# Weight residues on GpSimd, normed y on ScalarE, and one state layout for both heads of a pair

## The chip, the cores and the metric

The kernel runs on one core of a Trainium2 chip. A core has five engines with queues of their own: TensorE (PE, with PEld for its weight loads), VectorE (DVE), ScalarE (ACT), GpSimd (POOL) and SyncE (SP), which here issues the transfers. Engines wait for each other by semaphores, and each takes its own instructions in the order in which the program lists them. The metric is the device time of one execution in microseconds, as the median of a few runs.

## The reference

Three layers follow each other, all in float32. In the program the weights arrive as 64-bit words and are first turned into float32.

```python
# attention, for every batch b (4) and head h (8), over t = 0..767, head size 48
state = alpha[:, :, t, :, None] * state + einsum('bhd,bhe->bhde', k[:, :, t], v[:, :, t])
y[:, :, t] = einsum('bhd,bhde->bhe', q[:, :, t], state)
# x: the heads side by side, 3072 tokens x 384
xn = x / sqrt(mean(x * x) + 1e-06) * rms_g
g = xn @ w_gate                                  # 384 x 1536
x = (g * sigmoid(g) * (xn @ w_val)) @ w_out      # 1536 x 384
h = maximum(maximum(x @ w1, x @ w2), x @ w3)     # 384 x 768 each
return h @ w2_out                                # 768 x 384
```

## The kernel before

**Attention.** The 768 tokens of a batch are cut into 6 chunks c of 128; with 4 batches that makes 24 tiles (class `Tile_`), numbered n, chunk by chunk over the batches. In a tile the 8 heads lie in 4 pairs: one head of a pair on partitions 0 to 47, the other on 64 to 111. For the first six tiles PE transposes alpha, k and q (part `pa`, `pe_a`, line 570); later ones come in already cut so that DVE transposes them (`bt`). DVE forms running products of alpha by scans and scales k and q with them (`br`, `b`). PE makes the scores (`pb`, line 644, one PSUM bank for each head of a pair), DVE masks them (`c`, line 657), and PE forms the new state U (line 667) and y (part `pc`): from the old state by line 676, and from the masked scores by line 682. Tiles with c = 0 have no old state. The scaled old state `Sd` is 96 columns wide, with each head of the pair in its own half of the rows and of the columns and zeros elsewhere, so that one matmul of 112 rows serves both heads. ScalarE sums the squares of y (`ss`), POOL forms r = (mean + eps)^-0.5 (`rr`, lines 693 and 696), DVE updates the state (`st`) and makes the normed y, xn = y * r * g (`d`, line 710), PE transposes it (`pd`), and it is split into a high part xh (ScalarE, `eh`) and a residue xl (DVE, `el`).

**The split.** Every product of the two later layers is three matmuls in the fp32r type: high x high, high x residue, residue x high. A weight chunk of 128 x 384 (class `Weights`) is loaded by SP as 64-bit words, joined to float32 by three DVE instructions (lines 58 to 60), copied to its high part by ScalarE (`high`, line 374), and the residue is the difference of the two (`low`, line 380, on DVE). ScalarE also checks the range of the words (lines 389 and 392). There are 60 chunks, taken two at a time.

**Layers.** Blocks of 384 tokens (three tiles) go through the feed-forward layer in slots: gate and value products (line 760), their product on DVE (line 793), its split, and the second matmul (line 807). The last layer follows in the same way (lines 760 and 960).

**Order.** Nothing is ordered by hand: class `Order` simulates the engines with a cost and a due time for each part, and lists the instructions in the order in which its model starts them. Where its PE would stand idle ahead of the value product of slot 0 it places a dummy matmul (`fill`, line 767). After slot 0 has begun, three PSUM banks are left for attention. `ident`, the unit matrix that the transposes need, and `mask` are built on POOL by helpers (masks.py).

Of the kernel before, what the change touches and what calls it, by code (L numbers as in the profile page):

```python
# [11 lines left out]
F32 = mybir.dt.float32  # L12
# [6 lines left out]
ALU = mybir.AluOpType  # L19
# [262 lines left out]
def gla_moe_moe(ctx: ExitStack, tc: tile.TileContext, q, k, v, alpha, wg, wv, wo, g, w1, w2, w3, wo2, out):  # L282
# [27 lines left out]
    banks = [pp.tile([P, 512], F32, name=f"bank{i}") for i in range(8)]  # L310
# [11 lines left out]
    class Weights:  # L322


        def __init__(self, tag, pool, bufs, chunks, where, due, needs):

            self.tag, self.pool, self.raws, self.tmps = tag, pool, {}, {}
            self.chunks, self.where = chunks, where
            n = len(chunks)
            first = tag == "w1"  # L330
            for i in range(n):
                at = due(i) - 10 - (HEAD[i // 2] if first and i < 8 else 1.5)
                before = needs(i) + self.prev("load", i, 1) + self.prev("check", i, bufs)
                if i >= bufs:
                    before.append((tag, "join", (i - bufs) // 2 * 2))
                plan.add((tag, "load", i), "SP", 1.1, at, before, partial(self.load, i, bufs), later=LAT)
            for i in range(0, n, 2):
                both = [j for j in (i, i + 1) if j < n]
                at = due(i) - (HEAD[i // 2] if first and i < 8 else 1 if first else 1.5)
                plan.add((tag, "join", i), "DVE", 1.3 * len(both), at,  # L340
                         [(tag, "load", j) for j in both] + self.prev("rest", i, 2) + self.prev("join", i, 2),
                         partial(self.join, both))
                plan.add((tag, "high", i), "ACT", 0.42 * len(both), at, [(tag, "join", i)] + self.needed(needs, both),
                         partial(self.high, both))
                plan.add((tag, "rest", i), "DVE", 0.47 * len(both), at + 0.2, [(tag, "high", i)],
                         partial(self.low, both))
                for j in both:
                    plan.add((tag, "check", j), "ACT", 1.14, at + 2, [(tag, "load", j)],
                             partial(self.check, j))
# [81 lines left out]
    gb = ap1.tile([P, DM], F32, name="gb")  # L431
# [10 lines left out]
    Sds = [ap1.tile([W, NP, 2 * D], F32, name=f"Sd{s}") for s in range(2)]  # L442
    for t in (ends, starts, *Sds):
        nc.gpsimd.memset(t, 0.0)
# [3 lines left out]
    make_identity(nc, ident)  # L448
    make_upper_triangular(nc, mask, val=1.0, diag=True)
# [19 lines left out]

    def square(col, src, rows, n):  # L470
        nc.scalar.activation(junk[:rows, :n], src, AF.Square, accum_out=stats[:rows, col:col + 1])
# [4 lines left out]
    class Tile_:  # L476


        def __init__(self, n):
# [36 lines left out]
            add("br", "DVE", 1.6, 1, [t("pa" if self.pe else "bt")] + free, self.pre_br)  # L516
            add("b", "DVE", 2.1 if c else 1.8, 1, [t("br")] + ([t("st", n - B)] if c else []) +
                ([t("st", n - 2)] if n < NT - B + 2 else []), self.pre_bq)
            add("sqb", "ACT", 1.48, 1.5, [t("b")], self.post_b)
# [4 lines left out]
            add("c", "DVE", 1.25, 2, [t("pb"), t("pc", n - 1)], self.pre_c)  # L524
# [3 lines left out]
            add("ss", "ACT", 0.42, 3, [t("pc")], self.norm)  # L528
            add("rr", "POOL", 0.6, 3, [t("ss")], self.root)
            if not last:  # L530
                add("st", "DVE", 0.54, 3, [t("pc")], self.pre_st)
# [3 lines left out]
            add("eh", "ACT", 0.42, 4, [t("pd")], self.split_h)  # L535
            add("el", "DVE", 0.47, 4, [t("eh")], self.split_l)
# [93 lines left out]
        def pe_b(self):  # L630
            self.in_b = []
            self.sc = []
# [5 lines left out]
            for _ in HALVES:  # L638
                sc, j = take(self.n, P, NP, P)
                self.in_b.append(j)  # L640
                self.sc.append(sc)
            for pr in range(NP):
                for i, lo, hi in HALVES:
                    nc.tensor.matmul(  # L644
                        self.sc[i][:, pr, :], self.kT[lo:hi, pr, :], self.qT[lo:hi, pr, :], start=True, stop=True
                    )
# [6 lines left out]
        def pre_c(self):  # L653
            self.at = []
            for i in range(2):
                a_ = ap.tile([P, NP, P], F32, name="at", bufs=2)
                nc.vector.tensor_tensor(a_, self.sc[i], mask.unsqueeze(1).to_broadcast([P, NP, P]), ALU.mult)
                self.at.append(a_)
            give(self.in_b[-2:])

        def pe_c(self):
            vt, at = self.vt, self.at
            if self.c < NC - 1:
                self.U, self.in_u = take(self.n, W, NP, D)
                for pr in range(NP):
                    for i, lo, hi in HALVES:
                        nc.tensor.matmul(  # L667
                            self.U[lo:hi, pr, :], self.kn[:, pr, lo:hi], vt[:, 2 * pr + i, :],
                            start=True, stop=True, skip_group_check=True,
                        )  # L670

            self.y, self.in_y = take(self.n, P, H, D)
            for pr in range(NP):
                if self.c:
                    for tk in TOKENS:
                        nc.tensor.matmul(  # L676
                            self.y[tk, 2 * pr:2 * pr + 2, :].rearrange("p a d -> p (a d)"), self.qT[:, pr, tk],
                            Sds[self.s][:, pr, :], start=True, stop=False, skip_group_check=True,
                        )
                for i in range(2):  # L680
                    for tk in TOKENS:
                        nc.tensor.matmul(  # L682
                            self.y[tk, 2 * pr + i, :], at[i][:, pr, tk], vt[:, 2 * pr + i, :],
                            start=not self.c, stop=True, skip_group_check=True,
                        )
            self.y = self.y.rearrange("p h d -> p (h d)")

        def norm(self):
            square(self.c0 + 3, self.y, P, DM)
# [8 lines left out]
        def pre_st(self):  # L698
            for i, lo, hi in HALVES:
                if self.c:  # L700
                    nc.vector.tensor_tensor(
                        St[self.b][lo:hi], self.U[lo:hi], Sds[self.s][lo:hi, :, i * D:(i + 1) * D], ALU.add
                    )
                else:
                    nc.vector.tensor_copy(St[self.b][lo:hi], self.U[lo:hi])
# [12 lines left out]
        def split_h(self):  # L718
# [4 lines left out]
            nc.scalar.activation(xh[blk][:, :, j * P:(j + 1) * P], self.xt, AF.Copy)  # L723

        def split_l(self):
            sl = slice(self.j * P, (self.j + 1) * P)
            nc.vector.tensor_tensor(
                xl[self.blk][:, :, sl], self.xt, xh[self.blk][:, :, sl].bitcast(F32), ALU.subtract
            )
            give([self.in_d])  # L730

    def give(which):
        for i in which:
# [3 lines left out]
             lambda: nc.sync.dma_start(out=gb, in_=g.unsqueeze(0).to_broadcast([P, DM])), later=2.0)  # L737
# [312 lines left out]
```

## Time and profile before

| | us |
|---|---|
| median of 3 runs | 926.93 (926.07 to 927.68) |
| the profiled execution | 927.05 |
| its span | 925.2 |
| PE busy | 888.6 |
| DVE busy | 527.4 |
| ACT busy | 353.4 |
| POOL busy | 24.3 |

Busy time is the time in which an engine has at least one instruction under way. A matmul's record is longer than the time after which the next may start, so the distance of two starts says more than a duration. The clock in a table of windows is what PE was granted there: 1.00 is 2.4 GHz and 0.50 is 1.2 GHz. The rows on which the prediction rests stand further below.

### The profile page before, as it was taken

How to read it: one execution, taken by the hardware profiler on the slowest of the kernel's cores; microseconds unless marked ns; L12 is line 12 of the kernel's file. 1: busy time of each engine (PE TensorE's matmuls, PEld its weight loads, DVE VectorE, ACT ScalarE, POOL GpSimd, SP SyncE). 2: the span in 40 equal slices, each digit the busy share in tenths (PEclk: the TensorE clock that was granted, in tenths of full speed). 3: DMA queues.
4: the chain of work that ended last, by engine and by line, in shares of the span. 5: the costliest groups of instructions: out<-in, count | busy, mean ns of one | idle time of the engine just before them, and what ended most of it. 6: DMA issues, size and time to landing. Idle time of an engine off the chain costs nothing.

```text
span 925.2 us, 16299 instructions
## 1 busy us (share of the span) xinstructions
PE 888.6 (96%) x6477; PEld 864.7 (93%) x6477; DVE 527.4 (57%) x1052; ACT 353.4 (38%) x898; POOL 24.3 (3%) x70
## 2 busy tenths in 40 slices
PE   4899699899999999999999999999999999999997
PEld 3789699799999999999999999999999999999997
DVE  3999978987666666666666258465333323323222
ACT  3568577432333333333223258553222212212121
POOL 1001000000000000000000000000000000000000
PEclk9999799999999999999999999999999999999999
DMA  8745454533223223222221025221100101101000
GB/s 170 130 125 172 129 187 120 146 108 82 56 57 82 57 56 83 56 57 82 57 56 53 1 86 182 92 99 39 52 26 27 52 1 52 39 13 52 1 26 28
DMA packets 106241, 69.14 MB, mean 75 GB/s; under 512 B 49200, under 2 KB 103856, under 8 KB 106160
## 3 DMA queue, kind: packets, MB, share of 16 engines
q1 hardware_dynamic: 106160, 68.05, 26.8%
q8 instruction: 52, 0.85, 0.4%
q14 instruction: 29, 0.24, 0.1%
HBM read 57.41 MB, written 10.62 MB: 74 GB/s over the span
## 4 chain that ended last, share of the span: by engine, by line
PE 84%; DVE 7%; DMA 2%; ACT 1%; issue 1%; POOL 0%; SPq 0%; DVEq 0%; POOLq 0%; ACTq 0%
PE bank L760 53%; PE bank L807 14%; PE bank L960 8%; PE bank L644 2%; PE bank L682 2%; PE bank L676 2%; DMA raw<-in_moe_w_dram 1%; DMA raw<-in_moe_w_val_dram 1%; PE bank L667 1%; DVE cv_t L59 1%; PE bank L716 1%; DVE aT L611 1%; DVE cv_t L60 1%; PE bank L637 1%; DVE sg L793 1%
## 5 line engine op out<-in xcount | busy, mean ns | idle before, releaser
L945 DVE TENSOR_TENSOR sg<-sg,bank 128x384 f32<-128x384 f32 x96 | 53.2, 554 | 171.6 <-PE bank L760 168.3
L793 DVE TENSOR_TENSOR sg<-sg,bank 128x384 f32<-128x384 f32 x96 | 52.8, 551 | 104.2 <-PE bank L760 103.5
L797 ACT ACTIVATE hh<-sg 128x384 fp32r<-128x384 f32 x96 | 50.2, 523 | 150.6 <-DVE sg L793 150.5
L760 PE MATMUL bank<-xh,wvh 128*128 128x384 f32 x288 | 98.7, 343 | 7.3 <-DVE sg L793 4.3
L760 PE MATMUL bank<-xh,wgh 128*128 128x384 f32 x288 | 100.8, 350 | 0.0
L760 PE MATMUL bank<-xh,wvl 128*128 128x384 f32 x288 | 97.7, 339 | 1.6 <-DVE wvl L380 1.6
L760 PE MATMUL bank<-xh,wgl 128*128 128x384 f32 x288 | 97.2, 337 | 1.5 <-DVE wgl L380 1.5
L807 PE MATMUL bank<-hh,woh 128*128 128x384 f32 x288 | 98.5, 342 | 0.0
L807 PE MATMUL bank<-hl,woh 128*128 128x384 f32 x288 | 96.7, 336 | 1.8 <-DVE hl L801 1.8
L760 PE MATMUL bank<-xl,wvh 128*128 128x384 f32 x288 | 97.4, 338 | 0.0
L760 PE MATMUL bank<-xl,wgh 128*128 128x384 f32 x288 | 97.1, 337 | 0.0
L807 PE MATMUL bank<-hh,wol 128*128 128x384 f32 x288 | 96.4, 335 | 0.0
L949 ACT ACTIVATE hh<-sg 128x384 fp32r<-128x384 f32 x48 | 25.2, 525 | 160.2 <-DVE sg L945 160.2
L801 DVE TENSOR_TENSOR hl<-sg,hh 128x384 fp32r<-128x384 f32 x96 | 53.3, 555 | 32.1 <-ACT hh L797 32.1
L790 ACT ACTIVATE sg<-bank 128x384 f32<-128x384 f32 x96 | 46.6, 486 | 47.2 <-PE bank L760 46.7
L760 PEld LDWEIGHTS bank<-xh,wvh 128*128 128x128 f32 x288 | 54.8, 190 | 9.8 <-DVE sg L793 6.4
L760 PEld LDWEIGHTS bank<-xh,wvl 128*128 128x128 f32 x288 | 54.9, 191 | 2.2 <-DVE wvl L380 2.2
L807 PEld LDWEIGHTS bank<-hl,woh 128*128 128x128 f32 x288 | 54.1, 188 | 2.7 <-DVE hl L801 2.7
L760 PEld LDWEIGHTS bank<-xh,wgl 128*128 128x128 f32 x288 | 54.6, 190 | 1.8 <-DVE wgl L380 1.8
L807 PEld LDWEIGHTS bank<-hh,woh 128*128 128x128 f32 x288 | 54.2, 188 | 2.0
L760 PEld LDWEIGHTS bank<-xh,wgh 128*128 128x128 f32 x288 | 54.8, 190 | 1.3
L760 PEld LDWEIGHTS bank<-xl,wvh 128*128 128x128 f32 x288 | 54.9, 191 | 0.0
(137 smaller groups left out, 2004.3 us busy)
## 6 DMA issues: line engine op xcount, KB each, us to landing
raw<-in_moe_w_out_dram SPq DMA_DIRECT2D x18, 384.0 KB, 3.9
raw<-in_moe_w_dram SPq DMA_DIRECT2D x18, 384.0 KB, 3.9
y_scr<-yo SPq DMA_DIRECT2D x30, 192.0 KB, 2.0
raw<-in_moe_w_gate_dram SPq DMA_DIRECT2D x12, 384.0 KB, 4.0
vt<-in_v_dram SPq DMA_DIRECT2D x24, 192.0 KB, 2.6
raw<-in_moe_w_val_dram SPq DMA_DIRECT2D x12, 384.0 KB, 3.8
xl<-y_scr SPq DMA_DIRECT2D x8, 576.0 KB, 4.3
out_dram<-yo SPq DMA_DIRECT2D x24, 192.0 KB, 1.9
```

The source lines that it names most:

```text
L644: nc.tensor.matmul(self.sc[i][:, pr, :], self.kT[lo:hi, pr, :], self.qT[lo:hi, pr, :], start=True, stop=True)
L676: nc.tensor.matmul(self.y[tk, 2 * pr:2 * pr + 2, :].rearrange("p a d -> p (a d)"), self.qT[:, pr, tk], Sds[self.s][:, pr, :], start=True, ...
L682: nc.tensor.matmul(self.y[tk, 2 * pr + i, :], at[i][:, pr, tk], vt[:, 2 * pr + i, :], start=not self.c, stop=True, skip_group_check=True,)
L760: nc.tensor.matmul(ps, w_[:, kt, col], m_[:, kt, :], start=i == 0, stop=i == 3 * KT - 1)
L790: nc.scalar.activation(hid[s], banks[3][:, :NB], AF.Silu)
L793: nc.vector.tensor_tensor(hid[s], hid[s], banks[4][:, :NB], ALU.mult)
L797: nc.scalar.activation(hi_[s], hid[s], AF.Copy)
L801: nc.vector.tensor_tensor(lo_[s], hid.pop(s), hi_[s].bitcast(F32), ALU.subtract)
L807: nc.tensor.matmul(banks[e][:, :NB], w_[:, f, es], m_, start=f == f0 and i == 0, stop=f == f1 - 1 and i == 2)
L945: nc.vector.tensor_tensor(hid2[z], hid2[z], banks[3 + j][:, :NB], ALU.max)
L949: nc.scalar.activation(hi2[z], hid2[z], AF.Copy)
L960: nc.tensor.matmul(banks[t][:, :DM], l_[:, tsl], r_[:, f, :], start=f == 0 and i == 0, stop=f == NF2 - 1 and i == 2)
```

## The change

Six edits belong to it.

- Weight residues (`low`) are formed on POOL instead of DVE.
- Normed y is made by ScalarE as y * r; g is no longer a row broadcast over the partitions but a column per block of 128 features, and is multiplied in where y's transpose is split: three ScalarE instructions for xh and three DVE instructions for xl, one per block of features.
- The scaled state has 48 columns, in the layout of the state, for both heads of a pair. So its scaling and the update are one instruction each, and line 676's two matmuls of 112 rows become four of 48 rows (line 686).
- y takes two PSUM banks, one for each head of a pair; the scores of both heads are masked by one instruction. All banks are now views of one PSUM tile.
- `ident` and `mask` are built on DVE.
- Costs in the plan are changed, and with them the order.

```diff
-                plan.add((tag, "high", i), "ACT", 0.42 * len(both), at, ...
+                plan.add((tag, "high", i), "ACT", 0.45 * len(both), at, ...
-                plan.add((tag, "rest", i), "DVE", 0.47 * len(both), at + 0.2, [(tag, "high", i)],
+                plan.add((tag, "rest", i), "POOL", 1.0 * len(both), at + 0.2, [(tag, "high", i)],
...
-                nc.vector.tensor_tensor(
+                nc.gpsimd.tensor_tensor(
                     dl, self.tmps.pop(i).rearrange("p (a b) -> p a b", a=a), dh.bitcast(F32), ALU.subtract
                 )
...
-    Sds = [ap1.tile([W, NP, 2 * D], F32, name=f"Sd{s}") for s in range(2)]
+    Sds = [ap1.tile([W, NP, D], F32, name=f"Sd{s}") for s in range(2)]
...
-    make_identity(nc, ident)
-    make_upper_triangular(nc, mask, val=1.0, diag=True)
+    nc.vector.memset(mask, 1.0)
+    nc.vector.tensor_tensor_scan(column, mask, mask, -1.0, ALU.mult, ALU.add)
+    nc.vector.transpose(place, column[:, 0:32])
+    for t, op in ((ident, ALU.is_equal), (mask, ALU.is_ge)):
+        for lo in range(0, P, 32):
+            nc.vector.tensor_scalar(
+                t[lo:lo + 32], column[lo:lo + 32], float(lo), place[lo:lo + 32, 0:1], ALU.subtract, op
+            )
...
+    def take2(n, w):
+        i, j = sorted(take(n, P, 1, 1)[1] for _ in range(2))
+        return wall[:, i:j + 1:j - i, 0:NP * w].rearrange("p i (a n) -> p i a n", a=NP), [i, j]
...
             add("pc", "PE", (1.4 if c else 0.9) + (0 if last else 0.5), 2.5,
-                [t("c"), t("lv"), None if last else t("kn")], self.pe_c, banks=1 if last else 2,
+                [t("c"), t("lv"), None if last else t("kn")], self.pe_c, banks=2 if last else 3,
...
-            add("d", "DVE", 0.5, 3.1, [t("rr"), t("pc"), t("pd", n - 3), "gb"], self.pre_d)
+            add("d", "ACT", 0.5, 3.1, [t("rr"), t("pc"), t("pd", n - 3)], self.pre_d)
...
-                for i, lo, hi in HALVES:
-                    nc.vector.tensor_tensor(
-                        Sds[self.s][lo:hi, :, i * D:(i + 1) * D], St[self.b][lo:hi],
-                        self.all[lo:hi].to_broadcast([D, NP, D]), ALU.mult,
-                    )
+                nc.vector.tensor_tensor(Sds[self.s], St[self.b], self.all.to_broadcast([W, NP, D]), ALU.mult)
...
-                nc.vector.tensor_tensor(a_, self.sc[i], mask.unsqueeze(1).to_broadcast([P, NP, P]), ALU.mult)
+            nc.vector.tensor_tensor(
+                self.at, self.sc, mask.unsqueeze(1).unsqueeze(1).to_broadcast([P, 2, NP, P]), ALU.mult
+            )
...
                     for tk in TOKENS:
-                        nc.tensor.matmul(
-                            self.y[tk, 2 * pr:2 * pr + 2, :].rearrange("p a d -> p (a d)"), self.qT[:, pr, tk],
-                            Sds[self.s][:, pr, :], start=True, stop=False, skip_group_check=True,
-                        )
+                        for i, lo, hi in HALVES:
+                            nc.tensor.matmul(
+                                self.y[tk, i, pr, :], self.qT[lo:hi, pr, tk], Sds[self.s][lo:hi, pr, :],
+                                start=True, stop=False, skip_group_check=True,
+                            )
...
-            for i, lo, hi in HALVES:
-                if self.c:
-                    nc.vector.tensor_tensor(
-                        St[self.b][lo:hi], self.U[lo:hi], Sds[self.s][lo:hi, :, i * D:(i + 1) * D], ALU.add
-                    )
+            if self.c:
+                nc.vector.tensor_tensor(St[self.b], self.U, Sds[self.s], ALU.add)
...
-            nc.vector.scalar_tensor_tensor(self.xn, self.y, self.r[:, 1:2], gb, ALU.mult, ALU.mult)
-            give([self.in_y])
+            nc.scalar.activation(
+                self.xn.rearrange("p (a i d) -> p i a d", i=2, d=D), self.y, AF.Copy, scale=self.r[:, 1:2]
+            )
+            give(self.in_y)
...
-            nc.scalar.activation(xh[blk][:, :, j * P:(j + 1) * P], self.xt, AF.Copy)
+            for i in range(KT):
+                nc.scalar.activation(
+                    xh[blk][:, i, j * P:(j + 1) * P], self.xt[:, i, :], AF.Copy, scale=gt[:, i:i + 1]
+                )
...
+            for i in range(KT):
+                nc.vector.scalar_tensor_tensor(
+                    xl[self.blk][:, i, sl], self.xt[:, i, :], gt[:, i:i + 1], xh[self.blk][:, i, sl].bitcast(F32),
+                    ALU.mult, ALU.subtract,
+                )
...
-             lambda: nc.sync.dma_start(out=gb, in_=g.unsqueeze(0).to_broadcast([P, DM])), later=2.0)
+             lambda: nc.sync.dma_start(out=gt, in_=g.rearrange("(k p) -> p k", p=P)), later=2.0)
```

In the changed program lines from 438 on are numbered up to 15 higher: the products are line 773, `fill` is 780, the weight residues 381, y 686 and 692.

On PE, part `pc` of the first tile that has an old state stood like this before (U, then per pair of heads y from the state `Sd` and y from the masked scores `at`; `x` counts equal instructions in a row):

```order
L667 MATMUL bank_80<-vt,kn 48x48 x8
L676 MATMUL bank_78<-Sd_117,qT 64x96 x2
L682 MATMUL bank_78<-vt,at 64x48 x4
...
L716 MATMUL bank_79<-ident,xn 128x128 x3
L760 MATMUL bank_76<-xh,wgh 128x384
```

and stands like this now:

```order
L675 MATMUL bank<-vt,kn 64x48
L675 MATMUL bank<-vt,kn 48x48
...
L686 MATMUL bank<-Sd_110,qT 64x48 x4
L692 MATMUL bank<-vt,at 64x48 x4
...
L820 MATMUL bank<-hh,woh 128x384
```

The alternation per pair stays; there are four matmuls from the state where there were two, and they read 48 rows instead of 112.

On POOL, the end of the preparation and the first parts of the plan were, before:

```order
L446 MEMSET ends 112x4
masks.py:197 MEMSET ident 128x128
masks.py:199 ISA
masks.py:199 AFFINE_SELECT ident<-ident 128x128
masks.py:65 MEMSET mask 128x128
masks.py:66 AFFINE_SELECT mask<-mask 128x128
L450 MEMSET half 128x1
L693 TENSOR_SCALAR r<-stats 128x1
L696 TENSOR_TENSOR r<-r,half 128x1
```

and are now (`ISA` is a load of code for the instruction behind it):

```order
L447 MEMSET ends 112x4
L460 MEMSET half 128x1
L381 ISA
L381 TENSOR_TENSOR wgl<-cv_t,wgh 128x3x128
L381 TENSOR_TENSOR wvl<-cv_t,wvh 128x3x128
L702 TENSOR_SCALAR r<-stats 128x1
L705 TENSOR_TENSOR r<-r,half 128x1
L381 TENSOR_TENSOR wol<-cv_t,woh 128x384
```

The unit matrix has left POOL, the load of code has moved behind it, and the r of a tile now stands behind weight residues.

On DVE, ahead of the fourth tile (n = 3; its first parts begin with the copy into `all`), stood before normed y of an earlier tile and two weight residues:

```order
L710 SCALAR_TENSOR_TENSOR xn<-bank_79,r,gb 128x384
L380 TENSOR_TENSOR wol<-cv_t,woh 128x384
L380 TENSOR_TENSOR wgl<-cv_t,wgh 128x3x128
L595 COPY all<-bank_80 112x4
L596 MEMSET bank_80 112x4
L598 SCALAR_TENSOR_TENSOR R<-bank_80,ends 112x511
```

and the same place now reads:

```order
L632 TENSOR_TENSOR qT<-bank,aT 112x512
L711 COPY S_117<-bank 112x192
L610 COPY all<-bank 112x4
L611 MEMSET bank 112x4
L613 SCALAR_TENSOR_TENSOR R<-bank,ends 112x511
```

Normed y and the weight residues are gone from DVE's list.

## Rows read from the trace of the kernel before

**Rows 1.** Windows: stretch; length, busy us of each engine; clock, DMA share, GB/s.

```profile
0.00:13.65 13.65, 0.00 (x0) 0.00 (x1) 0.00 (x0) 3.96 (x9) 3.46 (x19) 1.00 0.94 196
13.65:56.70 43.05, 38.95 (x434) 34.09 (x435) 39.59 (x84) 21.78 (x65) 3.28 (x9) 0.96 0.65 131
56.70:96.00 39.30, 38.34 (x384) 35.37 (x381) 38.04 (x84) 31.05 (x87) 3.71 (x6) 1.00 0.49 142
96.00:115.00 19.00, 11.53 (x38) 10.69 (x38) 17.34 (x38) 10.42 (x31) 0.00 (x0) 0.64 0.54 145
115.00:184.00 69.00, 65.80 (x498) 63.20 (x497) 59.96 (x129) 44.82 (x121) 1.66 (x4) 1.00 0.52 153
...
sum 925.20, PE 888.55 PEld 864.70 DVE 527.37 ACT 353.40 POOL 24.32; mean PE 126.94 PEld 123.53 DVE 75.34 ACT 50.49 POOL 3.47
```

**Rows 2.** Waits in 0 to 46 us: who waited for what, us, times, longest.

```profile
PE bank L570 <- POOL ident masks.py:199: 13.7, 1, 13.7
...
POOL ident masks.py:199 <- issue: 9.6, 1, 9.6
```

**Rows 3.** Transfers issued in 0 to 16 us: count, size, median us to landing.

```profile
in_kk<-in_k_dram SPq DMA_DIRECT2D x3, 192.0 KB, 4.0
```

**Rows 4.** Timeline up to the first product: start, us, engine, line, tiles [idle before].

```profile
1.24 0.57 SPq L542 DMA_DIRECT2D in_kk<-in_k_dram  x1
...
30.90 2.67 PE L767 MATMUL bank<-mask,ident 128*128 128x256 bf16 x23
...
39.91 0.55 PE L716 MATMUL bank<-ident,xn 128*128 128x128 f32 x3 [1.39 <-DVE xn L710]
...
46.16 0.56 PE L667 MATMUL bank<-vt,kn 128*48 128x48 f32 x16 [2.48 <-issue]
...
56.72 0.42 PE L760 MATMUL bank<-xh,wgh 128*128 128x384 f32 x1
```

**Rows 5.** Windows 98.8 to 104.8 and 109.06 to 115 us, both at clock 0.50: their sum.

```profile
sum 11.94, PE 10.28 PEld 9.78 DVE 10.38 ACT 7.37 POOL 0.00; mean PE 5.14 PEld 4.89 DVE 5.19 ACT 3.69 POOL 0.00
```

**Rows 6.** Timeline of PE around one tile's U and y (part `pc`).

```profile
209.00 0.34 PE L760 MATMUL bank<-xh,wgl 128*128 128x384 f32 x1
209.26 0.56 PE L667 MATMUL bank<-vt,kn 128*48 128x48 f32 x16
209.66 0.35 PE L676 MATMUL bank<-Sd,qT 112*64 112x96 f32 x4
209.84 0.39 PE L682 MATMUL bank<-vt,at 128*64 128x48 f32 x8
...
211.04 0.39 PE L682 MATMUL bank<-vt,at 128*64 128x48 f32 x8
211.36 0.44 PE L807 MATMUL bank<-hh,woh 128*128 128x384 f32 x1
211.64 0.34 PE L807 MATMUL bank<-hl,woh 128*128 128x384 f32 x1
211.81 0.34 PE L807 MATMUL bank<-hh,wol 128*128 128x384 f32 x1
```

**Rows 7.** Window 56.7 to 115 us, weight residues alone (line 380).

```profile
56.70:115.00 58.30, 8.16 (x16) 0.88 0.51 143
```

**Rows 8.** Groups by line and shape: count, busy us, mean ns of one, idle before.

```profile
L710 DVE SCALAR_TENSOR_TENSOR xn<-bank,r,gb 128x384 f32<-128x384 f32 x24 | 14.7, 611 | 4.9 <-POOL r L696 4.3
...
L617 DVE TENSOR_TENSOR Sd<-S,all 48x192 f32<-48x192 f32 x40 | 13.6, 340 | 0.3
...
L444 POOL MEMSET starts<- 112x512 f32 x1 | 0.5, 524 | 0.0
```

**Rows 9.** Timeline: POOL's line 693 alone, and beside DVE's line 60.

```profile
26.19 0.19 POOL L693 TENSOR_SCALAR r<-stats 128x1 f32<-128x1 f32 x1 [12.02 <-ACT junk L471]
...
88.36 1.02 DVE L60 SCALAR_TENSOR_TENSOR cv_t<-raw,cv_t 128x384 int32<-128x384 int32 x2
...
88.40 1.03 POOL L693 TENSOR_SCALAR r<-stats 128x1 f32<-128x1 f32 x1 [9.43 <-ACT junk L471]
```

More of the change, by code (lines that the diff above doesn't have):

```diff
@@ L9 @@
 from concourse.bass import ds
-from concourse.masks import make_identity, make_upper_triangular
+from concourse.masks import make_identity
 F32 = mybir.dt.float32
@@ L309, in gla_moe_moe @@
     pp = work.enter_context(tc.tile_pool(name="pp", bufs=1, space=PSUM))
-    banks = [pp.tile([P, 512], F32, name=f"bank{i}") for i in range(8)]
+    wall = pp.tile([P, 8, 512], F32, name="bank")
+    banks = [wall[:, i, :] for i in range(8)]
     mp = work.enter_context(tc.tile_pool(name="mp", bufs=2, side="left"))
@@ L342, in __init__ @@
                          partial(self.join, both))
-                plan.add((tag, "high", i), "ACT", 0.42 * len(both), at, [(tag, "join", i)] + self.needed(needs, both),
+                plan.add((tag, "high", i), "ACT", 0.45 * len(both), at, [(tag, "join", i)] + self.needed(needs, both),
                          partial(self.high, both))
-                plan.add((tag, "rest", i), "DVE", 0.47 * len(both), at + 0.2, [(tag, "high", i)],
+                plan.add((tag, "rest", i), "POOL", 1.0 * len(both), at + 0.2, [(tag, "high", i)],
                          partial(self.low, both))
                 for j in both:
-                    plan.add((tag, "check", j), "ACT", 1.14, at + 2, [(tag, "load", j)],
+                    plan.add((tag, "check", j), "ACT", 1.42, at + 2, [(tag, "load", j)],
                              partial(self.check, j))
@@ L430, in gla_moe_moe @@
     half = ap1.tile([P, 1], F32, name="half")
-    gb = ap1.tile([P, DM], F32, name="gb")
+    gt = ap1.tile([P, KT], F32, name="gt")
     ins, halves = [], []
@@ L441, in gla_moe_moe @@
     starts = ap1.tile([W, NP, P], F32, name="starts")
-    Sds = [ap1.tile([W, NP, 2 * D], F32, name=f"Sd{s}") for s in range(2)]
-    for t in (ends, starts, *Sds):
+    Sds = [ap1.tile([W, NP, D], F32, name=f"Sd{s}") for s in range(2)]
+    for t in (ends, starts):
         nc.gpsimd.memset(t, 0.0)
@@ L447, in gla_moe_moe @@
     St = [ap1.tile([W, NP, D], F32, name=f"S{b}") for b in range(B)]
-    make_identity(nc, ident)
-    make_upper_triangular(nc, mask, val=1.0, diag=True)
+    column = ap1.tile([P, P], F32, name="column")
+    place = ap1.tile([P, 32], F32, name="place")
+    nc.vector.memset(mask, 1.0)
[6 more added lines that the diff above has]
+            )
     nc.gpsimd.memset(half, -0.5)
@@ L468, in room @@
         return count
+    def take2(n, w):
+        i, j = sorted(take(n, P, 1, 1)[1] for _ in range(2))
+        return wall[:, i:j + 1:j - i, 0:NP * w].rearrange("p i (a n) -> p i a n", a=NP), [i, j]
     def square(col, src, rows, n):
[L471 removed]
+        nc.scalar.activation(junk[:rows, :n] if isinstance(n, int) else n, src, AF.Square, accum_out=stats[:rows, col:col + 1])
     NPE = 6
@@ L515, in __init__ @@
                 add("bt", "DVE", 1.85, 0.9, [t("ld")] + free, self.pre_bt)
-            add("br", "DVE", 1.6, 1, [t("pa" if self.pe else "bt")] + free, self.pre_br)
-            add("b", "DVE", 2.1 if c else 1.8, 1, [t("br")] + ([t("st", n - B)] if c else []) +
+            add("br", "DVE", 2.3, 1, [t("pa" if self.pe else "bt")] + free, self.pre_br)
+            add("b", "DVE", 2.5 if c else 2.15, 1, [t("br")] + ([t("st", n - B)] if c else []) +
                 ([t("st", n - 2)] if n < NT - B + 2 else []), self.pre_bq)
-            add("sqb", "ACT", 1.48, 1.5, [t("b")], self.post_b)
+            add("sqb", "ACT", 1.95, 1.5, [t("b")], self.post_b)
             add("pb", "PE", 1.75 if last else 2.13, 1.5, [t("b"), t("pc", n - 1)], self.pe_b,
@@ L637, in pe_b @@
                     nc.tensor.transpose(self.kb[:, pr, :], self.kT[:, pr, :], ident[:W, :W])
[L638 to L641, printed above, removed]
+            self.sc, two = take2(self.n, P)
+            self.in_b += two
             for pr in range(NP):
@@ L644, in pe_b @@
                     nc.tensor.matmul(
-                        self.sc[i][:, pr, :], self.kT[lo:hi, pr, :], self.qT[lo:hi, pr, :], start=True, stop=True
+                        self.sc[:, i, pr, :], self.kT[lo:hi, pr, :], self.qT[lo:hi, pr, :], start=True, stop=True
                     )
@@ L653, in pre_c @@
         def pre_c(self):
-            self.at = []
-            for i in range(2):
-                a_ = ap.tile([P, NP, P], F32, name="at", bufs=2)
-                nc.vector.tensor_tensor(a_, self.sc[i], mask.unsqueeze(1).to_broadcast([P, NP, P]), ALU.mult)
-                self.at.append(a_)
+            self.at = ap.tile([P, 2, NP, P], F32, name="at", bufs=1)
+            nc.vector.tensor_tensor(
+                self.at, self.sc, mask.unsqueeze(1).unsqueeze(1).to_broadcast([P, 2, NP, P]), ALU.mult
+            )
             give(self.in_b[-2:])
@@ L665, in pe_c @@
                 for pr in range(NP):
-                    for i, lo, hi in HALVES:
+                    for i, lo, hi in ((0, 0, 64), (1, 64, W)):
                         nc.tensor.matmul(
@@ L670, in pe_c @@
                         )
-            self.y, self.in_y = take(self.n, P, H, D)
+            self.y, self.in_y = take2(self.n, D)
             for pr in range(NP):
```

26 lines of the change are left out of this document (10 added, 16 removed).

## The prediction, made before the changed kernel ran

> **What bounds the kernel now.** I read the table of windows first [rows 1]. It splits the span into a head, in which PE fills and feeds the first attention tiles, a middle in which DVE is nearly full, and a long rest in which PE is. PE is busy 888.55 us of 925.20 in all, and from 115 to 184 us it loses only 3.20 us. Everything that sets the end is therefore PE's stream: its own work, plus what it loses before about 184 us. So an edit counts in one of three ways: it lets PE begin sooner, it takes a loss away, or it changes the length of PE's own work.
>
> The head: PE's first transpose waits 13.7 us for `ident`, and POOL is late with it because of 9.6 us of "issue", in which it does nothing that the trace shows [rows 2]. From 13.65 us to the first product of the feed-forward layer at 56.72 us [rows 4] DVE is busy 39.59 of 43.05 us [rows 1], but PE is almost as full, because the plan puts dummy matmuls (line 767) wherever it expects a gap. PE really waits only twice there, 1.39 and 2.48 us [rows 4].
>
> The middle: from 56.7 to 115 us DVE is busy 38.04 of 39.30 and 17.34 of 19.00 us [rows 1]. PE stands idle 0.96 us in the first of these windows and 7.47 us in the second, and after its two longest waits it runs at a granted clock of 0.50, that is 1.2 GHz: 10.28 us of busy PE [rows 5], worth 5.14 us at 2.4 GHz. With the 3.20 us before 184 us, PE's losses behind the first product are 0.96 + 7.47 + 5.14 + 3.20 = 16.8 us.
>
> **Part 1, the start.** `ident` and `mask` come from 11 small DVE instructions. DVE has nothing to do before 14 us, so they cost nothing as long as they end before the inputs land: in_kk, which the second group of transposes reads, is issued at 1.24 us [rows 4] and lands 4.0 us later [rows 3], at 5.24. None of the 11 has more elements per partition than a third of a 128x384 DVE instruction, which takes 0.61 us [rows 8], so, begun with the kernel near 0.3 us, they end by 0.3 + 11 x 0.61 = 7.0 us at worst, 1.8 us late, and more likely near 3. POOL's code load stays in the order, now ahead of its first weight residue; PE no longer waits for it, and there are some 10 us before the first residue. So PE begins 13.65 - 5.24 = 8.4 us earlier. Three things take of that. The new order has 171 dummy matmuls before the first product where there were 141: 23 took 2.67 us [rows 4], 0.11 each after the tail, so 30 more are 3.3 us. PE's two waits (3.9 us) hang on DVE, which here loses the six residues that lie ahead of the first product, normed y and half of the state copies; I take 1.0 us to remain of them. One tile more is finished ahead of the first product; that moves the first product, but the same work is missing behind it, so it cancels. Net: -8.4 + 3.3 - 3.9 + 1.0 = **-8.0 us**. The bounds: nothing at all, if the second tile's loads (ends of the same queue, which is 0.94 busy in the first 13.65 us [rows 1]) hold up what PE gained, and -11.3 if the fillers cost nothing. g as a column instead of a broadcast takes 192 KB off that queue; I count it at nothing.
>
> **Part 2, the middle.** Between 56.7 and 115 us DVE does 16 residues, 8.16 us busy [rows 7]. They go to POOL. Normed y (0.611 each) goes to ScalarE, and the scaling and the update of the state become one instruction each instead of two of 0.340 us [rows 8]; with three tiles in that stretch, whose first has no state to scale, 3 x 0.61 + 5 x 0.34 = 3.5 us. The mask in one instruction instead of two saves a little, the residue of x in three instead of one costs a little (at most two whole instructions, 1.2 us a tile; at least nothing); I let these two cancel. Relief: about 11.7 us of 55.4. What comes late next is bounded by ScalarE, which gains 0.5 us a tile for y and some 0.4 for splitting x in three; it was busy 31.05 of 39.30 us [rows 1], so 3 tiles fit.
>
> What a residue costs on POOL the trace doesn't show. POOL writes 112x512 in 0.52 us [rows 8], so 384 columns are 0.39 for one pass; a residue reads twice and writes once, so 0.39 is the floor and 1.2 the ceiling, and I take 0.8. POOL has 60 of them and is busy 24.32 us in all [rows 1], so it has room. The worse question is whether the two engines hold each other up. They do: POOL's 128x1 instruction of line 693 takes 0.19 us alone, and 1.03 us when it starts beside DVE's line 60, which reads two SBUF operands; DVE's own duration doesn't change [rows 9]. So POOL's 0.8 us can start late by some 1 us, and it may in turn hold DVE. From nothing to 16 x 0.8 = 12.8 us of DVE time comes back; I take 4 us, since the rows show POOL as the one that waits. That leaves 7.7 us of relief in a queue whose lateness costs PE 13.6 us by 115 us, the half clock included; a queue that is 95% full gets rid of most of its lateness when a seventh of its work goes.
> The Trainium skill (SBUF — State Buffer, Who interferes with whom) says that a DVE instruction with two SBUF inputs and a GpSimd instruction that reads SBUF exclude each other, whoever comes second waiting in full. The 1.03 us row agrees; by that rule at its worst all 12.8 us come back, which is rival 3's time.
>
> One wait moves: POOL's r of a tile now stands behind up to two residues in its order, and normed y on ScalarE waits for r, with checks and weight copies queued behind it there; the transposes of y on PE wait for that. Two residues are 1.6 us, and on DVE the same place waited for r as well, so I count nothing for it outside the bounds.
>
> I take PE's losses behind the first product from 16.8 to 5.8 us: **-11.0 us**. Bounds: 0 and -15.
>
> **Part 3, y on PE.** This one is on the path in all 20 tiles with c > 0, because all lie behind the first product. Before, per pair of heads: L676 starts 0.18 us before L682, both on 64-column halves of the array, and a pair takes 0.40 us (L682 at 211.04 less that at 209.84, by three), so L682 takes 0.22 and passing from one to the other costs nothing [rows 6]. After: four quarter-size matmuls (48 rows) in place of two of 112, alternating with the unchanged full-height ones of line 692, so the array's split changes twice per pair, 8 times a tile. No row shows just this change of split, but others are there. From L760 (whole array) to L667 (halves) the next matmul starts 0.27 us later instead of about 0.17, so 0.09 us is lost; going back from L682 to L807, 211.36 against 211.04 + 0.22 loses 0.10 us and the second matmul, 0.28 after the first instead of 0.17, another 0.11 [rows 6]. So a change costs 0.09 at least and 0.21 at most; I take 0.14, as the weights here are half as wide as L807's. The quarter matmuls themselves: if four run side by side their 0.18 us shrinks to about half, if only two do it stays; I take 0.07 off. Per tile 4 x (2 x 0.14 - 0.07) = 0.83 us, times 20 = **+16.6 us**. Bounds: 20 x 4 x -0.09 = -7 with free changes, 20 x 4 x (2 x 0.21) = +34.
> The Trainium skill (TensorEngine Tiling (Array Packing), Tiling Modes) puts it as "Changing tiling mode (not just tile) drains the TensorE". The 0.09 and 0.10 us rows agree, between other pairs of modes. By the rule the 16.6 us stand; without a drain the sum is rival 1's.
>
> y now holds two PSUM banks instead of one, so at y all three free banks are taken; in the new order the next tile's scores stood behind y before too, so I count nothing. ScalarE has 22 us more over all tiles, and is busy 353.40 of 925.20 now [rows 1].
>
> **Sum.** -8.0 - 11.0 + 16.6 = -2.4 us on a span of 925.2, so 922.8; with 1.85 us around the span of this execution (927.05) that is **924.6 us**. The median of the three runs, 926.93, is 0.1 us below that execution.
>
> **Rivals.**
> 1. *The array's split costs nothing extra, and four quarters run together*: y gets shorter, 924.6 - 16.6 - 7 = 901. For it: passing from L667 to L676, other shapes on the same split, is free. Against: each of the two visible changes of split has its gap.
> 2. *The split costs what leaving it for L807 costs, 0.21*: 8 x 0.21 - 0.28 = 1.40 a tile, +28 in all, so 924.6 + 11.4 = 936; at 0.18 it is 931. Parts 1 and 2 give 19.0 us, 0.95 a tile; from (0.95 + 0.28) / 8 = 0.154 us a change on, y eats them and the kernel is slower. For it: all of L807's loss is visible. Against: its weights are twice as wide.
> 3. *POOL and DVE exclude each other in full*: DVE gets its 12.8 us back, the middle gains 2 us instead of 11 and the head 2 us less: 924.6 + 9 + 2 = 936. For it: the 1.03 us row. Against: there it is POOL that waits.
> 4. *The start doesn't move*, because tile 2's loads or the longer row of fillers hold the first product near 56 us: 924.6 + 4 to 8 = 929 to 933. For it: the queue at 0.94. Against: DVE has about 10 us of work on the first tile and the weights while those loads come.
>
> **How the numbers follow.** My forecast has 47% (917 to 932 by itself), rival 1 15%, rival 2 20%, rival 3 12%, rival 4 6%. About 0.2%, 1.9 us, is what a measurement of this kernel can tell from no change, so "same" is 925.1 to 928.8. Of the forecast's 47, 27 are faster, 13 same and 7 slower; rival 1 adds 15 to faster; rivals 2 to 4 add 34 to slower and 4 to same. Together 42, 17 and 41, with the likeliest time just on the faster side. The range 906 to 938 holds the forecast and most of rivals 2 to 4, and leaves out the better half of rival 1 and the far end of y's bound.
>
> **What would show it.** Part 1: PE's first transpose near 5 us and the first product near 51.5 (with the tile that moved ahead), no wait for `ident`. Part 2: DVE's busy share from the first product on falls, and PE's two long waits with the half clock behind them are gone; line 381 on POOL near 0.8 us; a DVE duration over 0.6 us at lines 59 and 60 would speak for rival 3. Part 3: from the first row of line 686 to the end of line 692 a tile takes 2.4 us where L676 to L682 took 1.6; gaps of 0.1 us and more between each 686 and 692 prove the drain, and 1.6 or less proves rival 1. A first product at 56 us or PE losses above 10 us behind it make the forecast wrong, whatever the sum is.

## The result and the profile after

The changed kernel takes 939.66 us (median of 4 runs, 939.34 to 940.10) against 926.50 us for the kernel before beside it. The ratio is 1.0141, with a 95% interval of 1.0123 to 1.0159: 1.4% slower, where 924.6 us and a range of 906 to 938 were forecast.

The windows of the changed kernel, in the columns of [rows 1]:

```profile
0.00:13.65 13.65, 9.51 (x76) 7.97 (x76) 11.27 (x26) 5.75 (x15) 2.42 (x15) 1.00 1.05 189
13.65:56.70 43.05, 34.15 (x449) 29.41 (x448) 32.06 (x68) 26.02 (x80) 8.98 (x12) 1.00 0.71 138
56.70:96.00 39.30, 34.84 (x341) 31.18 (x339) 33.49 (x67) 29.34 (x84) 12.37 (x16) 1.00 0.60 165
96.00:115.00 19.00, 14.12 (x78) 12.96 (x79) 17.40 (x39) 14.29 (x43) 5.43 (x5) 0.91 0.54 155
115.00:184.00 69.00, 67.40 (x506) 65.18 (x505) 50.03 (x103) 42.94 (x119) 19.74 (x20) 0.95 0.46 132
sum 938.00, PE 908.16 PEld 876.64 DVE 488.64 ACT 373.06 POOL 86.99; mean PE 151.36 PEld 146.11 DVE 81.44 ACT 62.18 POOL 14.50
```

DVE is relieved, but less than was meant in the middle: it has 32.06 us in the second window where it had 39.59, 33.49 in the third where it had 38.04, and 17.40 in the fourth where it had 17.34. So between 56.7 and 115 us it does 4.5 us less, where 11.7 were forecast. Yet PE, which now starts at 4.01 us, is busy only 34.15 of 43.05 us in the second window (before: 38.95) and 34.84 of 39.30 in the third (before: 38.34). And over the whole span PE has 19.6 us more to do (908.16 against 888.55). So the loss has two parts: PE waits in the head, where the waiting should have gone, and PE's own work has grown.

The first part, in the list of what PE waited for:

```profile
PE bank L585 <- DMA in_al<-in_alpha_dram: 4.0, 1, 4.0
PE bank L780 <- ACT xn L716: 3.0, 3, 1.5
PE bank L780 <- DVE at L663: 2.7, 2, 1.4
PE bank L652 <- DVE xl L739: 1.9, 1, 1.9
PE bank L675 <- ACT kn L658: 1.7, 1, 1.7
PE bank L675 <- DVE at L663: 1.6, 1, 1.6
PE bank L780 <- ACT junk L486: 1.4, 2, 0.7
...
PE bank L773 <- ACT xn L716: 1.2, 1, 1.2
...
PE bank L724 <- DVE at L663: 1.1, 1, 1.1
...
PE bank L773 <- ACT junk L486: 0.7, 1, 0.7
```

Line 780 is the dummy matmul. It writes bank 4, reads `ident` and `mask`, and needs nothing from anybody; before, none of the 141 waited. Now seven wait, 7.1 us in all, for the mask of the scores (line 663) and for the two reads of y (lines 486 and 716). The same seen in time, from the timeline of all engines:

```profile
18.06 0.28 PE L780 MATMUL bank<-mask,ident 128*128 128x256 bf16 x1
18.43 0.49 ACT L486 ACTIVATE junk<-bank 128x384 bf16<-128x384 f32 x1 [1.13 <-issue]
19.06 2.45 PE L780 MATMUL bank<-mask,ident 128*128 128x256 bf16 x21 [0.72 <-ACT junk L486]
...
20.07 0.77 POOL L705 TENSOR_TENSOR r<-r,half 128x1 f32<-128x1 f32 x1
...
21.61 0.58 ACT L716 ACTIVATE xn<-bank,r 128x384 f32<-128x384 f32 x1 [2.60 <-PE bank L780]
...
22.24 0.60 PE L780 MATMUL bank<-mask,ident 128*128 128x256 bf16 x4 [0.73 <-ACT xn L716]
...
57.83 0.44 PE L773 MATMUL bank<-xh,wgh 128*128 128x384 f32 x1 [0.72 <-ACT junk L486]
```

They wait for each other in turn: dummy, square of y, 21 dummies, normed y, dummies. The normed y has its r at 20.84 us and starts at 21.61, when the 21 dummies end. The first product, at 57.83 us, waits in the same way for a square of y that doesn't touch its bank. In the built program y lies here in banks 3 and 5, read in one instruction with a stride of two banks; the waits that the program sets treat that as a use of bank 4 too. All PSUM is now one tile, `wall`, and a two-bank view is kept apart from others as if it held everything from its first to its last address. Eight of the dummies' waits in the built program join an access to two such banks with one to bank 4 between them, and there are more such waits on PE, DVE and ACT; the kernel before, with a tile per bank, has none.

The second part, PE around U and y of one tile:

```profile
232.73 0.67 PE L675 MATMUL bank<-vt,kn 128*64 128x48 f32 x16
233.33 0.33 PE L686 MATMUL bank<-Sd,qT 48*64 48x48 f32 x8
233.59 0.44 PE L692 MATMUL bank<-vt,at 128*64 128x48 f32 x8
233.96 0.33 PE L686 MATMUL bank<-Sd,qT 48*64 48x48 f32 x8
234.22 0.44 PE L692 MATMUL bank<-vt,at 128*64 128x48 f32 x8
...
235.48 0.44 PE L692 MATMUL bank<-vt,at 128*64 128x48 f32 x8
235.85 0.44 PE L773 MATMUL bank<-xh,wgh 128*128 128x384 f32 x1
```

A pair takes 0.63 us (233.96 less 233.33) where it took 0.40 [rows 6], and y 2.52 us (233.33 to 235.85) instead of 1.70. U, from its first matmul to the first of y, takes 0.60 instead of 0.40.

Laid out by the starts of PE's single matmuls, the span grows by 12.8 us in these pieces: the start −9.64; the dummies 17.5 to 20.5 us, +3.0; waits ahead of the first product 4.10 to 9.75, +5.65; y +16.2 and U +3.6; waits behind the first product 13.04 to 10.26, −2.8; the rest of PE's work, mostly the products of line 773 (540.8 to 538.8 us), −3.1.

The half clock has moved rather than gone. Behind the first product PE is busy 10.24 us at a granted clock of 0.50, where it was 10.28 [rows 5]: the mean rises from 0.64 to 0.91 between 96 and 115 us and falls from 1.00 to 0.95 behind that. The windows 103.06 to 106.47 and 171.32 to 178.15 us of the changed kernel sum to:

```profile
sum 10.24, PE 10.24 PEld 9.82 DVE 7.69 ACT 4.44 POOL 3.46; mean PE 5.12 PEld 4.91 DVE 3.85 ACT 2.22 POOL 1.73
```

Only a stretch in the head, 46.8 to 50.2 us before, is gone; it cost half of its 3.4 us, 1.7, and part of that is in the −3.1.

### The profile page after: what moved, and what is told of

It reads as the page before. It is cut to its first block, busy times and chain, and to the rows that moved or that the text cites. A ratio compares the mean times of both kernels' runs of the same rounds, so it can differ in the third digit from the quotient of the medians.

```text
span 938.0 us, 17053 instructions
## 1 busy us (share of the span) xinstructions
PE 908.2 (97%) x6827; PEld 876.6 (93%) x6827; DVE 488.6 (52%) x963; ACT 373.1 (40%) x970; POOL 87.0 (9%) x124
## 4 chain that ended last, share of the span: by engine, by line
PE 92%; DVE 4%; ACT 2%; issue 1%; POOL 0%; DVEq 0%; ACTq 0%
PE bank L773 56%; PE bank L820 16%; PE bank L973 8%; PE bank L692 3%; PE bank L652 2%; PE bank L686 2%; PE bank L780 1%; PE bank L675 1%; PE bank L724 1%; PE bank L647 1%; DVE at L663 1%; ACT junk L486 1%; DVE R L613 1%; PE bank L585 0%; DVE cv_t L59 0%
## 5 line engine op out<-in xcount | busy, mean ns | idle before, releaser
L814 DVE TENSOR_TENSOR hl<-sg,hh 128x384 fp32r<-128x384 f32 x96 | 55.3, 576 | 44.8 <-ACT hh L810 44.5
L803 ACT ACTIVATE sg<-bank 128x384 f32<-128x384 f32 x96 | 46.8, 488 | 54.1 <-PE bank L773 54.0
```

Of the source, the lines that this page charges most:

```text
L803: nc.scalar.activation(hid[s], banks[3][:, :NB], AF.Silu)
L814: nc.vector.tensor_tensor(lo_[s], hid.pop(s), hi_[s].bitcast(F32), ALU.subtract)
```

## Experiments

**e1: y regrouped.** The quarter matmuls of all four pairs first, then all full-height ones. As run, the start flags of the later pairs leave the state's part of y out for three pairs of four; the instructions are the same.

```
-            for pr in range(NP):
-                if self.c:
+            if self.c:
+                for pr in range(NP):
                     for tk in TOKENS: ...
+            for pr in range(NP):
                 for i in range(2):
```

> The changed kernel, with y's quarter matmuls of all four pairs ahead of all of the full-height ones: two changes of the array's split per tile instead of eight, same matmuls. Theory A (the change of split costs 0.10 us each way and another 0.04 for the first matmuls behind it): a pair's 0.63 us falls to about 0.15 + 0.22, a tile's y from 2.5 to 1.7 us, 20 tiles give 12 to 16 us: time 924 to 928. Rival (the quarter matmuls or the two banks themselves are slow): y stays above 2.2 us and the time above 935.

923.98 us, ratio to the kernel before 0.9972 (0.9961 to 0.9984). The same stretch of PE:

```profile
228.12 0.67 PE L675 MATMUL bank<-vt,kn 128*64 128x48 f32 x16
228.72 0.68 PE L686 MATMUL bank<-Sd,qT 48*64 48x48 f32 x32
229.33 1.14 PE L693 MATMUL bank<-vt,at 128*64 128x48 f32 x32
230.40 0.44 PE L774 MATMUL bank<-xh,wgh 128*128 128x384 f32 x1
```

y takes 1.68 us with the very same 64 records: 0.84 us of 2.52 were the six changes of the array's split, 0.14 each. By single starts (medians), the first quarter comes 152 ns behind the last full-height matmul, where full-height pairs follow each other at 52, and the second group of quarters 74 ns behind the first instead of 38: 0.136 us in. The first full-height matmul comes 149 ns behind the last quarter, where groups of quarters follow at 38, and the next pair 87 instead of 52: 0.146 us out. Theory A holds.

**e2: neighbouring banks.** The changed kernel with pairs of banks that are always neighbours; order of instructions unchanged.

```
-        i, j = sorted(take(n, P, 1, 1)[1] for _ in range(2))
...
+        free = [i for i in order if i in usable and i not in held]
+        pairs = [(i, i + 1) for i in free if i + 1 in free]
...
+        i, j = min(pairs, key=lambda p: max(order.index(x) for x in p))
```

(A single bank is chosen so that two free neighbours stay; the program then has no wait of that kind.)

> The changed kernel, with the two banks of a pair always neighbours and the single bank never between them; program order unchanged. Theory B (an access to banks 3 and 5, or 0 and 7, counts as one to all banks between, so that dummy matmuls in bank 4 and the reads of y and the scores wait for each other): PE's waits ahead of dummy matmuls (7.1 us in eight waits) and at least 4 us of those behind the first product go, the first product comes at 49 to 52 us instead of 57.8, time 928 to 932. Rival (the dummy matmuls only stand where PE would have waited for VectorE or ScalarE anyway): the waits move to the attention matmuls, first product at 55 us or later, time 935 to 940.

929.70 us, 1.0034 (1.0022 to 1.0045), 10.0 us less than the changed kernel. The dummies run through, and the transposes of the third tile stand 1.8 us earlier than at 22.68:

```profile
18.05 3.01 PE L789 MATMUL bank<-mask,ident 128*128 128x256 bf16 x26
20.90 0.60 PE L594 MATMUL bank<-ident,in_al 128*112 128x128 f32 x4
```

PE's waits ahead of the first product go from 9.75 to 2.76 us, behind it from 10.26 to 7.20: 10.05 together, as much as the gain of the medians. The profiled execution took 932.23 us, the longest of twelve; its span is only 7.5 us shorter, because PE's own work took 2.2 us more there (it was busy 13.2 us at half clock behind the first product). The first product comes at 52.19 us instead of 57.83. Theory B holds, with two bounds narrowly missed: 3.1 us of the waits behind the first product went where at least 4 were expected, and 52.19 lies just above 52. The rival, that dummies only stand where PE would have waited anyway, is out.

**e3: both edits** (with e1's start flags).

> The changed kernel with both edits: regrouped y and neighbouring banks. Theories A and B together, if their gains add up: 939.7 less 12 to 16 less 8 to 11, so 913 to 920, below the kernel before (926.5). If B's rival holds: 922 to 927. If A's rival holds: 928 or more.

914.71 us, 0.9879 (0.9856 to 0.9901). The gains add up: 939.66 − 15.7 − 10.0 = 914.0.

**e4: the unit matrix alone.** The kernel before, with only `ident` and `mask` made on DVE.

```
-    make_identity(nc, ident)
-    make_upper_triangular(nc, mask, val=1.0, diag=True)
+    nc.vector.memset(mask, 1.0)
+    nc.vector.tensor_tensor_scan(column, mask, mask, -1.0, ALU.mult, ALU.add)
...
```

> The kernel before, with only the unit matrix and the mask made on VectorE; its order of instructions on PE is unchanged (141 dummy matmuls ahead of the first product). Theory C (the late unit matrix bounds the head): PE starts near 4 us, the first product comes at 47 to 50 us instead of 56.7, time 917 to 921. Rival D (VectorE, nearly full from 13.65 us on, bounds the head, or the loads of the second tile do): first product at 53 to 56 us, time 923 to 926. The prediction's own term was in between: 8.4 us less some 1 us of a remaining wait.

918.90 us, 0.9918 (0.9898 to 0.9937): 7.7 us. PE starts at 4.12 us, 9.5 earlier, and the first product at 48.20, 8.5 earlier:

```profile
48.20 0.44 PE L768 MATMUL bank<-xh,wgh 128*128 128x384 f32 x1 [0.73 <-DVE xl L735]
```

Theory C holds. Of the 9.5 us that PE starts sooner, 1.0 is lost again ahead of the first product and 0.8 behind it.

**e5: both edits, mended.** `start=pr == 0` in place of `start=True` at the quarter matmuls, so that all of y is computed.

> Regrouped y and neighbouring banks as in the earlier run of both, but only the first pair's quarter matmuls carry the start flag (as run before, the later pairs' start flags left the state's part of y out for three pairs of four). Nothing else changes, so both theories expect the same: 913 to 917, y at 1.68 us a tile, first product near 50.6 us. If the flag costs time by itself, more.

912.74 us, 0.9850 (0.9833 to 0.9867): 1.5% faster than the kernel before, and just under the 913 to 917 that were expected. The start flag costs no time that these medians show.

**e6: residues back on DVE** in the mended kernel.

```
-                nc.gpsimd.tensor_tensor(
+                nc.vector.tensor_tensor(
                     dl, self.tmps.pop(i)...
```

(and in the plan "DVE", 0.47 instead of "POOL", 1.0)

> The same kernel with the 60 weight residues back on VectorE (0.51 us each) instead of GpSimd (1.0 us each). Theory E (the residues on GpSimd relieve a VectorE that sets PE's waits between 56 and 115 us): PE's waits and half clock come back in part, 3 to 8 us slower, 918 to 923. Rival F (the relief came from normed y, the mask and the state, and GpSimd's longer residue makes its own waits): within 2 us, 913 to 917.

911.47 us, 0.9838 (0.9817 to 0.9859), not to be told from e5. Theory E falls. F's figure of "within 2 us" holds, though the time lies under its range; where the relief came from instead, which F also says, this run doesn't show. The edit with the largest price in the forecast's relief, 8.16 of 11.7 us of DVE, moves nothing that these medians can tell.

**e7: quarters ahead of U** in the mended kernel: U and the full-height matmuls have the same split, so a change a tile goes.

> The mended kernel with the quarter matmuls of y put ahead of U: the array's split then goes whole, quarters, halves, whole instead of whole, halves, quarters, halves, whole, three changes a tile instead of four. Theory A (each change costs 0.11 us, and what is gained is on the path): 20 tiles x 0.11 to 0.15 = 2.2 to 3 us faster than the mended kernel, 911 to 914. Rival (the cost of a change depends on the pair of splits, and the one from whole to quarters costs the two together): no difference, 913 to 917.

912.68 us, 0.9851 (0.9834 to 0.9869): no difference, where theory A had 2.2 to 3 us. By single starts the step between U and y's second part costs nothing now and U and y are 1.4 us shorter in all; what of that reached the end these runs can't tell.

**e8: normed y back on DVE** in the mended kernel (`nc.vector.tensor_scalar` of y by r).

> The mended kernel with normed y on VectorE (0.61 us or less, without g) instead of ScalarE. Theory E (VectorE's load sets PE's waits): 6 tiles x 0.5 us more VectorE work ahead of 115 us costs 1 to 3 us. Rival G (normed y on ScalarE stands behind weight copies and checks and is late there; on VectorE it is earlier): 1 to 2 us faster. Neither: within 1 us.

924.83 us, 0.9979 (0.9969 to 0.9989): 12.1 us slower, which neither theory had. The longest wait of PE, with DVE ahead of it:

```profile
79.11 0.55 POOL L715 TENSOR_TENSOR r<-r,half 128x1 f32<-128x1 f32 x1
79.39 0.55 PE L656 MATMUL bank<-ident,kT 112*128 112x112 f32 x4
79.49 1.10 DVE L600 STREAM_TRANSPOSE qT<-in_qq 128x512 f32<-128x512 f32 x1
80.41 0.62 DVE L58 TENSOR_SCALAR cv_t<-raw 128x384 int32<-128x384 int32 x2
80.93 1.02 DVE L59 SCALAR_TENSOR_TENSOR cv_t<-raw,cv_t 128x384 int32<-128x384 int32 x2
81.87 1.02 DVE L60 SCALAR_TENSOR_TENSOR cv_t<-raw,cv_t 128x384 int32<-128x384 int32 x2
82.81 0.62 DVE L726 TENSOR_SCALAR xn<-bank,r 128x384 f32<-128x384 f32 x1
83.48 0.94 PE L661 MATMUL bank<-qT,kT 48*128 48x128 f32 x12 [3.55 <-DVE xn L726]
```

r is there at 79.66 us, but normed y stands behind a transpose and a join of weights until 82.81, and PE's scores wait for its banks. What these rows show is not DVE's load but the place of the one instruction that frees y's banks, in a queue with long neighbours. It is one wait of several: of the 11.1 us between the profiled spans of e8 and e5, 5.4 are waits of PE and 5.6 its own work, which ran 17.0 us at a granted clock of 0.50 instead of 6.6 (10.4 us more, worth 5.2).

**e9: both back on DVE**, residues and normed y.

> The mended kernel with both moved works back on VectorE: the weight residues and normed y. It tells why normed y on VectorE alone cost 12 us. Theory H (there normed y on VectorE waited for r, which stood behind 1.0 us residues on GpSimd, and held VectorE's queue): with the residues off GpSimd that wait goes, 911 to 917. Rival I (VectorE's own queue is what is late: weight joins stand ahead of normed y, y's banks stay held and the next scores wait): no better, 921 to 928.

918.11 us, 0.9911 (0.9894 to 0.9927): between H and I. Normed y on DVE costs 6.6 us with the residues on DVE (e9 less e6; the kernel before took 926.83 and 926.56 us beside them) and 12.1 with them on POOL (e8 less e5). DVE's waits of normed y for r up to 184 us, first in e8 and then in e9, agree with H for part of it:

```profile
DVE xn L726 <- POOL r L715: 4.7, 5, 2.9
```

```profile
DVE xn L726 <- POOL r L715: 2.2, 3, 1.0
```

The planner makes a new order for e6, e8, e9 and e10, so a part of the differences may be the order's; that stays open.

**e10: quarters ahead of U, and residues on DVE.**

> The best parts together: neighbouring banks, quarter matmuls ahead of U, residues on VectorE, normed y on ScalarE. Each of the last two edits came out within the noise of the mended kernel (912.7); their profiled spans were 2.7 and 3.5 us shorter. If both are small gains: 907 to 911. If neither is: 911 to 914.

914.44 us, 0.9860 (0.9836 to 0.9883). e5, e6, e7 and e10 lie within 3 us of each other, with intervals that overlap; the two small gains that the profiled spans had shown are not borne out, and the time is just above both ranges.

## Why the prediction was wrong

**The steps that failed.** Two terms of the sum were wrong. The first stands at the end of part 3: "y now holds two PSUM banks instead of one [...] so I count nothing." It was weighed as a question of how many banks are free. What it does is to make the banks between the two wait, and that costs 10.0 us (e2). With this term at 10.0 instead of 0, 924.6 becomes 934.6, and with U's 3.6 us, which the sum left out, 938.2; the run gave 939.7.

The second is part 2's size: PE's losses behind the first product were to fall from 16.8 to 5.8 us. Counted in the same way, they fell to 15.3 (10.2 us without work and half of 10.24 at half clock). That 938.2 still comes near the measured time is therefore partly luck: gains that the forecast didn't have made up for most of it.

**Part 1**, −8.0 expected. The start came 9.64 us sooner (8.4 expected; `in_al`, not `in_kk`, is the first group's input and lands at 4.0), the 30 more dummies took 3.0 us (3.3). But PE's waits ahead of the first product rose by 5.65 us instead of falling by 2.9, and the part came to −1.0. 7.0 of this is the banks' (9.75 to 2.76 in e2); without them it is −8.0. e4 alone, which has neither the extra dummies nor a relieved DVE, gives −7.7. So the mechanism and its size were right, and the gain was given back in the same stretch. The first product, 51.5 expected, came at 57.83, which the text had named as the sign against it; with neighbouring banks it is 52.19.

**Part 2**, −11.0 expected. By the forecast's own count, losses up to 184 us, it is −1.4 (16.77 to 15.34), and the sign that it had named against itself, losses above 10 us, came. The banks explain little of this: with neighbouring banks the losses are 13.8 us in e2's profiled execution, and 12.3 in e5. Neither the size nor the reason held. The forecast took PE's losses as DVE's share of a full queue, with the residues as its largest piece; but residues on either engine give the same time (e5, e6), and normed y, 0.61 us a tile, is worth 6.6 to 12.1 us (e9, e8). That this is because it holds banks that PE needs next is seen at one wait of 3.55 us and not shown for the rest, and what sets the other losses stays open.

POOL's residue takes 1.01 us (0.8 taken, within 0.39 to 1.2), and up to 1.99 beside DVE. Here the two do hold each other up, from both sides:

```profile
L381 POOL TENSOR_TENSOR wol<-cv_t,woh x12: 998/1014/1991, 25.9 to 168.7; 128x384 fp32r<-128x384 f32 x12
```

```profile
L625 DVE TENSOR_TENSOR all<-all,least x20: 130/131/893, 47.5 to 503.3; 112x4 f32<-112x4 f32 x20
...
L59 DVE SCALAR_TENSOR_TENSOR cv_t<-raw,cv_t x60: 543/551/556, 10.3 to 645.7; 128x384 int32<-128x384 int32 x60
```

These are the shortest, median and longest ns of a line in the changed kernel. A DVE instruction of 0.13 us with two SBUF inputs takes 0.89 when it starts 0.87 us before the end of a residue:

```profile
161.06 1.36 POOL L381 TENSOR_TENSOR wol<-cv_t,woh 128x384 fp32r<-128x384 f32 x1 [5.93 <-ACT woh L375]
161.54 0.89 DVE L625 TENSOR_TENSOR all<-all,least 112x4 f32<-112x4 f32 x1
```

DVE's lines 59 and 60, which the prediction had named as the sign, stay at 0.55; but in this trace none of them runs beside a residue, so they tell nothing of rival 3. The Trainium skill (SBUF — State Buffer, Who interferes with whom) states that whoever comes second waits in full; the 0.89 and 1.99 us rows agree. Rival 3 priced it at 936, close to the time measured, but e6 speaks against it as the cause: in the mended kernel, taking the residues off POOL gave 911.5 against 912.7.

**Part 3**, +16.6 expected for y, 0.83 us a tile: measured 0.82 (1.70 to 2.52), 16.2 us over all. (The forecast's own terms, 4 x 0.21, give 0.84 and 16.8; the slip is small.) The change of split costs 0.136 and 0.146 us by direction, 0.14 expected. The Trainium skill (TensorEngine Tiling (Array Packing), Tiling Modes) has it that a change of mode drains the engine; e1's y with two changes instead of eight agrees. Rival 2 is out by that, and of rival 1 one half is true: four quarters start within about 20 ns and a group of four follows each 58 ns. What was missed is U: its last step now passes to quarters (152 instead of 39 ns), and its matmuls, now with unequal halves of 64 and 48 columns, follow each other less evenly; 0.18 us a tile, +3.6.

**The balance.** Forecast −8.0 −11.0 +16.6 = −2.4; measured +12.8 on the profiled spans. Of the 15.2 us between, part 1 has 7.0 (all of it the banks'), part 2 9.6 (16.8 to 15.3 instead of 5.8), U 3.6 and y −0.4. The remaining −4.6 lie where the forecast had no term: waits behind 184 us −1.4, and −3.2 in the rest of PE's stream, of which the half clock of the head has at most 1.7; the other half these runs don't explain. So the banks' 10.0 us (e2) and U's 3.6 come near the whole difference only because what part 2 lost beyond the banks' share was mostly won elsewhere. The chances on faster and slower were almost equal, so the sum's sign rested on a term of nothing.

## What to carry to other kernels

A tile that spans several banks is one object to whatever sets the waits: a strided view of it may be tied to everything between its first and last address, so choose neighbours, and look whether an instruction that needs nothing waits. Matmuls that use different splits of the array belong in groups by split, not alternating. When an engine looks full, ask which of its instructions holds what the next engine needs; here the place of one 0.6 us instruction a tile was worth more than that of 60 residues.

## What the runs showed that was not expected

- Normed y's place is worth 12.1 us with the residues on POOL and 6.6 us with them on DVE, though its work is 24 x 0.61 us on an engine that is busy about half the time.
- The waits between dummies and reads went both ways: the dummies, put there so that PE doesn't idle, delayed the square and the norm of y (normed y ready at 20.84 us, started at 21.61), and so the real work.
- Four quarter matmuls side by side cost 58 ns a group, so a y of 32 quarter and 32 full-height records takes 1.68 us, as long as before (1.70) with 16 larger ones; the narrower state layout costs y nothing once it is grouped.
